# A transformer block on one core: seven instead of eight down products in the later periods of the first token half, and ScalarE accumulating part of them

## The chip, the cores and the metric

The kernel runs on one core of one Trainium2 chip. A core has five engines that run at once and each take their instructions in order: TensorE (PE, matmuls; its weight loads appear as PEld), VectorE (DVE), ScalarE (ACT), GpSimd (POOL) and SyncE (SP, which here only issues DMAs; ScalarE issues some too, shown as ACTq). The metric is the device time of one execution in microseconds (us). The profile is one more execution, recorded instruction by instruction.

## What is computed

A block of batch 1, 2048 tokens, width 576, hidden width 4608, everything in fp32: an attention part and then a gated feed-forward part, each behind a layer norm whose scale and shift come from a small conditioning vector.

```
x = A_x
h = layernorm(x) * (1 + ca) + sa
x = x + ga * attention(h)            # 32 heads, 4 segments of 512, with a memory between segments
h = layernorm(x) * (1 + cb) + sb
x = x + gb * ((silu(h @ w_gate) * (h @ w_up)) @ w_down)
```

The change lies in the feed-forward part and in the step from the attention part to it.

## The kernel before

**Numbers.** TensorE works in a reduced fp32 format. So each operand is split into a high and a low part (a ScalarE cast to the high part, then a VectorE subtraction for the low part), and a product is three matmuls: high by high, high by low, low by high.

**Order.** The feed-forward part (from line 1645) is written out by hand under a manual schedule: each engine runs its instructions in the order in which the Python code emits them. It works on two token halves, `t` = 0 and 1, of 1024 tokens, as two blocks of 512. For each half it goes through `NPR` = 18 periods, `p` = 0 to 17; a period takes 256 of the 4608 hidden columns. A period has 14 steps, `k` = 0 to 13.

**Gate and up.** Weights (two column blocks by two halves of 288 rows) times tokens (two halves of 288 by two blocks) is a 2 by 2 block product. It is done with seven block products instead of eight, for gate (`z` = 0) and up (`z` = 1): 14 products, one per step, `prod` (L1422), seven matmuls of 512 columns each. `step` (L1462) follows each by its evacuation: `copy_t` and silu on ScalarE, `fin` (L1438) mostly on VectorE. The step's weights were cast five steps before (`prep_w`, L1389: a ScalarE cast and a VectorE subtraction). In half 0, step 7 takes two `prep_w` and step 8 none: the loop of line 1756 has a bound that is one larger there.

**Down.** The four activation blocks of a period are multiplied by the down weights during the next period, `prev`. There are two forms.
- `plain` (L1545): the eight block products, as 8 chunks of 12 matmuls of 288 columns, in steps 4 to 11 of half 0. VectorE adds each chunk (128 x 576) to an accumulator in SBUF. The operands are four activation blocks (`prep_a`) and four weight blocks (`prep_d`).
- `down` (L1530): seven products as 14 chunks of 6 matmuls, spread by `CH` over steps 0 to 12 (two chunks in steps 4 and 11, none in 6 and 13). VectorE adds each chunk to one of seven accumulators `acc[1..7]`. The operands are seven activation sums (`sum_a` on VectorE in steps 2 to 5) and seven weight blocks (`sum_d`). At the end `comb` (L1574) adds the accumulators up, eight adds of 128 x 1152.

`is_plain` (L1579) decides: half 0 is plain throughout, half 1 uses the seven products in periods 0 to 15 and is plain in 16 and 17. The chunks of both use two PSUM buffers `dn` in turn. The seven weight sums of half 1 are made in half 0 by GpSimd (`mul_d` in steps 4 and 5, `sum_d` in steps 6 to 9) and stored to DRAM for half 1 (line 1821, issued by ScalarE in step 12).

**Operands of half 1.** While half 0 runs, the generator `prep2` (L1262) makes the normed, transposed and split tokens of half 1: row loads, layer norm, transposes on TensorE (into the same `dn` buffers), scale and shift, block sums on GpSimd, splits, stores to DRAM. The main loop calls it once per step in steps 1 to 13 (line 1863) of every period from 1 on; what is left is run when period 17 begins.

**Remainder rows.** 32 rows of each 288 are packed apart. For two periods at a time they are loaded (`load_rb`), summed (`sum_rb`, GpSimd), split (`split_rb`, step 4), stored to DRAM by three DMAs that ScalarE issues (`store_rb`, L1377, step 6 of odd periods) and read back as `wr` by SyncE (`prep_r`, L1357).

**From attention to feed-forward** (lines 1661 to 1715). The last quarter of the output projection (`wo_m`, L861; `wo_x`, L876, VectorE adds its result to x) runs in 32 small pieces `n`, while the first operands arrive: four operand loads `load_y` of more than 1 MB each are queued on SyncE before. GpSimd runs the weight sums, memsets and the four `sum_rb(0, ...)` (n = 7 to 10); ScalarE casts (n = 12), and the subtraction follows on VectorE; `store_rb` at n = 14, `prep_r` at n = 18 and 19. The first product needs `wr`.

Of the kernel before, what the change touches and what calls it, by code (L numbers as in the profile page):

```python
# [7 lines left out]
F32 = mybir.dt.float32  # L8
# [42 lines left out]
LM = 3  # L51
G2 = range(1, 14)
WC = 4
PRIME = (0, 1, 3, 2, 5, 4, 7, 6) + tuple(range(8, 14))
# [50 lines left out]
def block(ctx: ExitStack, tc: tile.TileContext, x, wqk, wv, wo, beta, wgu, wrm, wd, c, w_mod, wm01, out):  # L105
# [1156 lines left out]
    def prep2(x2p):  # L1262
# [17 lines left out]

        xl = ha.rearrange("p a b -> p (a b)")[:, :D]
        for sn, i in ((2, 3), (3, 0), (3, 1), (3, 2), (3, 3)):
            nc.sync.dma_start(xl, xD[sn][:, i, :])
            for _ in range(5):
                yield
# [12 lines left out]
            nc.sync.dma_start(xhD[sn][:, i, :], xl)  # L1298
            yield
        for kb in range(3):  # L1300
            n = P if kb < 2 else 96
            for hv in range(2):
                for kh in range(2):
                    c0 = 288 * kh + 128 * kb
                    for b in range(2):
                        src = xhD[2 + b][:, 2 * hv:2 * hv + 2, c0:c0 + min(P, 288 - 128 * kb)]
                        if kb < 2:
                            nc.sync.dma_start(xb[:, 2 * b:2 * b + 2, :], src)
                        else:
                            for j in range(3):  # L1310
                                nc.sync.dma_start(xb[:, 2 * b:2 * b + 2, 32 * j:32 * j + 32], src)
                    for _ in range(3 if kb < 2 else 5):
                        yield
                    pt = ps.tile([P, 2, L], F32, tag="dn", name="pt", bufs=2)[:, 0].rearrange("p (a b) -> p a b", b=P)
                    for i in range(4):
                        nc.tensor.transpose(pt[:n, i, :], xb[:, i, :n], ident)
# [3 lines left out]
                    yield  # L1320
                h00, h10, h01, h11 = [ha[:n, k, 256 * b:256 * b + 256] for k in range(2) for b in range(2)]
                nc.gpsimd.tensor_tensor(t3[:n], h11, h10, op=ALU.subtract)
# [45 lines left out]
    def sum_rb(j, i):  # L1368
        sum_w(RB[j], i, nc.gpsimd)

# [135 lines left out]

    PA, acc, x11 = {}, {}, {}
    NS = [4] + [7] * (NPR - 3) + [4] * 2
# [15 lines left out]
    def store(t, b, h, src, c=None):  # L1524
# [3 lines left out]
                          src[:, i0:i1])  # L1528

    def down(t, p, c):  # L1530
        m, c = POS[c // 2], c % 2
        ah, al = AP[p % 2, m]
        dh, dl = DP[p % 2, m]
        pd = ps.tile([P, 2, L], F32, tag="dn", name="pd", bufs=2)
        for i in range(2):
            tk = slice(128 * (2 * c + i), 128 * (2 * c + i) + 128)
            for k, (a, w) in enumerate(((ah, dh), (ah, dl), (al, dh))):
                nc.tensor.matmul(pd[:, i, :288], lhsT=a[:, tk], rhs=w, start=(k == 0), stop=(k == 2))  # L1538
        o = acc[m][:, 2 * c:2 * c + 2]
        if p == 0 and m not in (2, 3, 4):  # L1540
            nc.vector.tensor_copy(o, pd[:, :, :288])
        else:
            nc.vector.tensor_tensor(o, o, pd[:, :, :288], op=ALU.add)  # L1543
# [29 lines left out]

    def comb(j):  # L1574
        d, b = ((2, 1), (0, 5), (6, 1), (5, 6), (3, 5), (7, 6), (4, 7), (0, 7))[j]
        d = acc[d] if d else x11[1]
        nc.vector.tensor_tensor(d, d, acc[b], op=ALU.add)

    def is_plain(t, p):  # L1579
        return t == 0 or p >= NPR - 2  # L1580

# [18 lines left out]
    with tc.manual_schedule():  # L1600
# [79 lines left out]
        for i in range(4):  # L1680
            for h in range(2):
                for c in range(WC):
# [8 lines left out]
                    if n == 6:  # L1691
                        for z in range(2):
                            nc.gpsimd.memset(f32(R[z][96:128]), 0.0)
                        for o in ACT_OP.values():
                            nc.gpsimd.memset(f32(y[96:128, o, 4]), 0.0)
                    if 7 <= n < 11:
                        sum_rb(0, n - 7)
                    elif n == 12:
                        split_rb(0)
                    elif n == 14:  # L1700
                        store_rb(0)
                    elif n in (18, 19):
                        prep_r(0, 0, n - 18)
                    if n == 24:
# [18 lines left out]
        p6 = ExitStack()  # L1723
        new_acc(accp, (2, 3, 4, 5))
        load_d(0, 0)
        seq = [(p, z, m) for t in range(2) for p in range(NPR) for z in range(2) for m in MP]
# [8 lines left out]
        for t in range(2):  # L1735
            for p in range(NPR):
# [4 lines left out]
                if t == 0 and p == 1:  # L1741
                    p7.close()
                    x2p = pool(p6, "x2p")
                    g2 = prep2(x2p)
                if t == 0 and p == NPR - 1:
                    run(g2)
                    p6.close()
                    accq = pool(p4, "acq")
                    new_acc(accq, (1, 6, 7))
                if last:  # L1750
                    load_x11(1)
                chunk = 0
                for k in range(14):
# [8 lines left out]
                    while acts:  # L1762
                        acts.pop(0)()
                    if dl and k in HP:
                        y_here(6 + HP.index(k))
# [16 lines left out]
                    else:  # L1782
# [15 lines left out]
                        elif dl and k in (6, 7):  # L1798
                            mul_d(p, k - 6, nc.vector)
                        elif not dl and k in (4, 5):  # L1800
                            mul_d(p, k - 4)
                        if dl and 9 <= k < 13:
                            for j in (0, 1):
# [30 lines left out]
                    elif prev is not None:  # L1834
# [8 lines left out]
                        for _ in range(CH[k]):  # L1843
                            down(*prev, chunk)
                            chunk += 1
                    if last and 1 <= k < 9:
                        comb(k - 1)
                    if p == 0 and (t, k) in RS:
# [5 lines left out]
                    elif k >= 7:  # L1854
                        if p == 0 and k < 9:
# [78 lines left out]
```

## Time and profile before

| | |
|---|---|
| three runs | 1802.44, 1805.81, 1807.12 us (median 1805.81) |
| the profiled execution | 1806.4 us, its span 1804.5 us |
| granted TensorE clock, mean | 0.996 |
| busy share of the span | PE 98%, PEld 84%, DVE 78%, ACT 51%, POOL 26% |
| DMA | 309.84 MB, mean 172 GB/s |
| end of the attention part, first feed-forward product | the product starts at 550.87 us |
| feed-forward half 0, periods 1 to 17 | about 576 to 1176 us |
| feed-forward half 1 | about 1176 to 1804 us |

How to read it: a row of the engine table is time in which the engine had an instruction running. Matmuls overlap, so the time from one start to the next tells more than the length of one. "SPq" and "ACTq" rows are DMA issues, which are not counted as busy but hold the queue of their engine.

The second half of the page's strips (40 slices of 45 us) for the feed-forward part reads 9 throughout for PE, 7 to 8 for DVE in half 0 and 8 to 9 in half 1, 3 to 5 for ACT, and for POOL 3 to 5 in half 0 and 0 in half 1.

### The profile page before, as it was taken

What the parts mean: (1) busy time and instruction counts of PE and PEld (TensorE: products, weight loads), DVE (VectorE), ACT (ScalarE), POOL (GpSimd) and SP (SyncE); (2) the same over time, 40 slices, a digit from 0 to 9 for tenths busy, and PEclk for the clock granted to TensorE, in tenths of its full rate; (3) what the DMA queues carried; (4) which work ended last, traced back from release to release, by engine and by line L of the source; (5) the groups of instructions that cost most, each with busy time, mean ns of one, the idle gap of its engine ahead of it and who ended that gap; (6) DMA issues with size and microseconds to landing.
All of it is one profiled execution on the core that took longest, in us unless ns stands there. A gap on an engine that the chain in (4) does not pass through costs nothing.

```text
span 1804.5 us, 31293 instructions
## 1 busy us (share of the span) xinstructions
PE 1774.5 (98%) x11053; PEld 1511.6 (84%) x11053; DVE 1403.4 (78%) x3215; ACT 924.0 (51%) x2010; POOL 469.0 (26%) x752
## 2 busy tenths in 40 slices
PE   8999999999989999999999999999999999999999
PEld 5888866767767888888888888888888888888888
DVE  7567588999967776777777776568888888898886
ACT  6344577778855444444444443344544544544542
POOL 2100146555680443454353443100000000000000
PEclk9999999999998999999999999999999999999999
DMA  8678765577668555555654553594324324324331
GB/s 304 223 239 280 235 197 177 171 196 213 194 215 290 167 193 193 183 189 165 211 167 147 185 161 130 178 302 144 106 81 131 108 80 131 108 80 131 108 104 53
DMA packets 149188, 309.84 MB, mean 172 GB/s; under 512 B 28184, under 2 KB 60376, under 8 KB 147240
## 3 DMA queue, kind: packets, MB, share of 16 engines
q1 hardware_dynamic: 134824, 253.98, 46.4%
q10 hardware_dynamic: 14208, 53.86, 7.6%
q8 instruction: 88, 1.44, 0.3%
q14 instruction: 68, 0.56, 0.1%
HBM read 193.73 MB, written 113.33 MB: 170 GB/s over the span
## 4 chain that ended last, share of the span: by engine, by line
PE 79%; DMA 3%; DVE 2%; POOL 1%; issue 0%; ACT 0%; SPq 0%; ACTq 0%; DVEq 0%; POOLq 0%
PE A L1429 25%; PE pd L1557 14%; PE C L1429 13%; PE pd L1538 10%; PE B L1429 6%; PE av L766 3%; PE pw L874 2%; PE s L711 2%; PE s L740 2%; DMA y<-yD 1%; PE pn L1010 1%; DVE junk L211 1%; PE px L788 1%; PE pw L951 1%; DMA woraw<-in_wo_dram 0%
## 5 line engine op out<-in xcount | busy, mean ns | idle before, releaser
L1429 PE MATMUL A<-y,wh 128*128 128x512 f32 x1152 | 404.0, 391 | 0.7 <-DMA y<-yD 0.5
L1429 PEld LDWEIGHTS A<-y,wh 128*128 128x128 f32 x1152 | 216.7, 188 | 41.0 <-ACT sg L1445 0.7
L1567 DVE TENSOR_TENSOR acc<-acc,pd 128x576 f32<-128x576 f32 x156 | 117.5, 753 | 161.6 <-PE pd L1557 160.4
L1394 DVE TENSOR_TENSOR wl<-O,wh 128x256 fp32r<-128x256 f32 x504 | 235.3, 472 | 5.2 <-ACT wh L1393 4.7
L211 DVE CUSTOM_DVE_ANT_0 junk<-s,tri 128x384 bf16<-128x384 f32 (+3 forms) x512 | 218.5, 486 | 23.3 <-PE s L711 9.5
L1429 PE MATMUL A<-y,wl 128*128 128x512 f32 x576 | 224.7, 390 | 0.0
L1543 DVE TENSOR_TENSOR acc<-acc,pd 128x576 f32<-128x576 f32 x216 | 162.3, 752 | 54.8 <-PE pd L1538 49.7
L1429 PE MATMUL C<-y,wh 128*128 128x512 f32 x576 | 203.2, 393 | 0.0
L1393 ACT CAST wh<-O 128x256 fp32r<-128x256 f32 x504 | 197.4, 405 | 3.1 <-DVE xr L879 1.5
L1557 PE MATMUL pd<-dh,ah 128*128 128x288 f32 x640 | 189.8, 297 | 0.5 <-DVE x L1561 0.5
L1557 PE MATMUL pd<-dh,al 128*128 128x288 f32 x640 | 188.2, 294 | 0.0
L1557 PE MATMUL pd<-dl,ah 128*128 128x288 f32 x640 | 188.1, 294 | 0.0
L1498 ACT CAST ah<-sg 128x512 fp32r<-128x512 f32 x192 | 119.4, 622 | 68.6 <-DVE sg L1453 63.2
L1384 POOL TENSOR_TENSOR O<-O 128x256 f32<-128x256 f32 x132 | 108.9, 839 | 146.1 <-DMA O<-in_wgu_dram 59.2
L747 ACT ACTIVATE Pt<-s 128x512 f32<-128x512 f32 x256 | 135.5, 599 | 22.0 <-PE s L740 12.2
L1499 DVE TENSOR_TENSOR al<-sg,ah 128x512 fp32r<-128x512 f32 x192 | 136.6, 712 | 11.2 <-ACT ah L1498 10.7
L1538 PE MATMUL pd<-dh,ah 128*128 128x288 f32 x448 | 132.9, 297 | 0.0
L1538 PE MATMUL pd<-dl,ah 128*128 128x288 f32 x448 | 131.9, 294 | 0.0
L1538 PE MATMUL pd<-dh,al 128*128 128x288 f32 x448 | 131.2, 293 | 0.0
L1557 PEld LDWEIGHTS pd<-dl,ah 128*128 128x128 f32 x640 | 121.1, 189 | 6.7
L1557 PEld LDWEIGHTS pd<-dh,ah 128*128 128x128 f32 x640 | 120.2, 188 | 6.8 <-DVE x L1561 0.8
L1429 PEld LDWEIGHTS C<-y,wh 128*128 128x128 f32 x576 | 108.0, 188 | 19.4
(415 smaller groups left out, 4251.1 us busy)
## 6 DMA issues: line engine op xcount, KB each, us to landing
wr<-rD SPq DMA_DIRECT2D x213, 112.0 KB
O<-in_wgu_dram SPq DMA_DIRECT2D x36, 512.0 KB
O<-oD SPq DMA_DIRECT2D x36, 512.0 KB
oD<-O ACTq DMA_DIRECT2D x34, 512.0 KB
ks<-kD SPq DMA_DIRECT2D x64, 216.0 KB
qs<-qD SPq DMA_DIRECT2D x64, 216.0 KB
O<-in_wgu_dram SPq DMA_DIRECT2D x36, 384.0 KB
y<-yD SPq DMA_DIRECT2D x11, 1024.0 KB
```

The costliest lines, as they stand in the source:

```text
L211: nc.vector.tensor_tensor_reduce(junk[:, :n], bank[:, o:o + n], tri[:, L - n:], 1.0, -3e38, op0=ALU.add, op1=ALU.max, accum_out=mcol[u][0] ...
L747: nc.scalar.activation(pt[:, h], bank, AF.Exp, scale=SCALE)
L1384: eng.tensor_tensor(o[:, d], o[:, a], o[:, b], op=op)
L1393: nc.scalar.copy(wh, o)
L1394: later.append(lambda: nc.vector.tensor_tensor(wl, o, f32(wh), op=ALU.subtract))
L1429: nc.tensor.matmul(bank, lhsT=a, rhs=b, start=(first and n == 0), stop=(n == 6), skip_group_check=not first)
L1498: nc.scalar.copy(ah, src)
L1499: later.append(lambda: nc.vector.tensor_tensor(al, src, f32(ah), op=ALU.subtract))
L1538: nc.tensor.matmul(pd[:, i, :288], lhsT=a[:, tk], rhs=w, start=(k == 0), stop=(k == 2))
L1543: nc.vector.tensor_tensor(o, o, pd[:, :, :288], op=ALU.add)
L1557: nc.tensor.matmul(pd[:, i, :288], lhsT=a[:, tk], rhs=w, start=(k == 0), stop=(k == 5))
L1567: nc.vector.tensor_tensor(o, o, pd[:, :, :288], op=ALU.add)
```

## The change

1. In half 0 the down product uses the form with seven products from period `P7` = 7 to period 15 (nine periods); 0 to 6 and 16, 17 stay plain. Accumulators 1, 6 and 7 are allocated at period 7 instead of 17, half 0 gets an accumulator of its own for product 5 (`acc5[0]`), and `comb` now also runs in period 17 of half 0.
2. In half 0, five of the 14 chunks (`PA7` = 1, 3, 7, 9, 13) are accumulated without VectorE: at the start of the chunk's step ScalarE copies the accumulator into the PSUM buffer (`down_new`), the matmuls add to it, and ScalarE copies the result back. In the first use of a new accumulator there is nothing to copy in.
3. In those periods `mul_d` moves from steps 4 and 5 to step 2, `sum_d` from steps 6 to 9 to steps 3 and 4.
4. `prep2` must be done before period 7: it is called twice per step in periods 1 to 6, its loads use two buffers in turn and are issued further ahead, and the waiting steps between are fewer.
5. Before the feed-forward part, `sum_rb(0, ...)` runs on VectorE at n = 9, the cast at n = 10, the store at n = 12, `prep_r` at n = 17 and 18.

The diff, without the body of `prep2` (whose numbers of steps are told in the prediction where they are used):

```diff
+P7 = 7
+PA7 = (1, 3, 7, 9, 13)
...
     def sum_rb(j, i):
-        sum_w(RB[j], i, nc.gpsimd)
+        sum_w(RB[j], i, nc.gpsimd if j else nc.vector)
...
+    def down_acc(t, c):
+        m, c = POS[c // 2], c % 2
+        return (acc5[t] if m == 5 else acc[m])[:, 2 * c:2 * c + 2]
+
+    def down_new(t, p, c):
+        pd = PD[c] = ps.tile([P, 2, L], F32, tag="dn", name="pd", bufs=2)
+        if t == 0 and c in PA7 and (p > P7 or POS[c // 2] in (2, 3, 4)):
+            nc.scalar.copy(pd[:, :, :288], down_acc(t, c))
+
     def down(t, p, c):
-        m, c = POS[c // 2], c % 2
+        m, q = POS[c // 2], c % 2
         ah, al = AP[p % 2, m]
         dh, dl = DP[p % 2, m]
-        pd = ps.tile([P, 2, L], F32, tag="dn", name="pd", bufs=2)
+        pd = PD.pop(c)
+        new = p == (0 if t else P7) and m not in (2, 3, 4)
+        on_act = t == 0 and c in PA7
+        first = new or not on_act
...
-                nc.tensor.matmul(pd[:, i, :288], lhsT=a[:, tk], rhs=w, start=(k == 0), stop=(k == 2))
-        o = acc[m][:, 2 * c:2 * c + 2]
-        if p == 0 and m not in (2, 3, 4):
+                nc.tensor.matmul(pd[:, i, :288], lhsT=a[:, tk], rhs=w, start=(first and k == 0), stop=(k == 2),
+                                 skip_group_check=not first)
+        o = down_acc(t, c)
+        if on_act:
+            nc.scalar.copy(o, pd[:, :, :288])
+        elif new:
             nc.vector.tensor_copy(o, pd[:, :, :288])
...
     def is_plain(t, p):
-        return t == 0 or p >= NPR - 2
+        return p >= NPR - 2 or t == 0 and p < P7
...
-                    if 7 <= n < 11:
-                        sum_rb(0, n - 7)
+                    if n == 9:
+                        for j in range(4):
+                            sum_rb(0, j)
+                    elif n == 10:
+                        split_rb(0)
                     elif n == 12:
-                        split_rb(0)
-                    elif n == 14:
                         store_rb(0)
-                    elif n in (18, 19):
-                        prep_r(0, 0, n - 18)
+                    elif n in (17, 18):
+                        prep_r(0, 0, n - 17)
...
-                if t == 0 and p == NPR - 1:
+                if t == 0 and p == P7:
                     run(g2)
                     p6.close()
                     accq = pool(p4, "acq")
                     new_acc(accq, (1, 6, 7))
+                    acc5[0] = xp.tile([P, 4, 288], F32, tag="xs", name="acc50")
...
                     while acts:
                         acts.pop(0)()
+                    if prev is not None and not is_plain(*prev):
+                        for j in range(CH[k]):
+                            down_new(*prev, chunk + j)
...
-                        elif not dl and k in (4, 5):
+                        elif not dl and is_plain(t, p) and k in (4, 5):
                             mul_d(p, k - 4)
+                        elif not is_plain(t, p) and k in (2, 3, 4):
+                            for j in (0, 1):
+                                if k == 2:
+                                    mul_d(p, j)
+                                else:
+                                    sum_d(p, 2 * k - 6 + j)
...
-                        if not dl and k in (6, 7, 8, 9) and p < NPR - 2:
+                        if not dl and k in (6, 7, 8, 9) and p < P7:
                             sum_d(p, k - 6)
...
-                    if last and 1 <= k < 9:
-                        comb(k - 1)
+                    if p == NPR - 1 and 1 <= k < 9:
+                        comb(t, k - 1)
...
-                    if t == 0 and k in G2 and p > 0:
+                    if t == 0 and k in G2 and 0 < p < P7:
+                        next(g2, None)
                         next(g2, None)
```

More of the change, by code (lines that the diff above doesn't have):

```diff
@@ L1279, in opr, with load_row @@
             yield
[L1281 to L1285, printed above, removed]
+        xl2 = x2p.tile([P, D], F32, tag="xl2", name="xl2")
+        xls = (ha.rearrange("p a b -> p (a b)")[:, :D], xl2)
+        rows = ((2, 3), (3, 0), (3, 1), (3, 2), (3, 3))
+        def load_row(j):
+            sn, i = rows[j]
+            nc.sync.dma_start(xls[j % 2], xD[sn][:, i, :])
+        load_row(0)
+        load_row(1)
+        for _ in range(5):
+            yield
+        for j, (sn, i) in enumerate(rows):
+            xl = xls[j % 2]
             st = x2p.tile([P, 2, 6], F32, tag="st3", name="st3")
@@ L1299, in prep2, with load @@
             yield
+            if j < 3:
+                load_row(j + 2)
+            for _ in range(3):
+                yield
+        xbs = (xb, xl2[:, :L].rearrange("p (a b) -> p a b", b=P))
+        def load(j):
+            kb, hv, kh = j // 4, j // 2 % 2, j % 2
+            c0 = 288 * kh + 128 * kb
+            for b in range(2):
+                src = xhD[2 + b][:, 2 * hv:2 * hv + 2, c0:c0 + min(P, 288 - 128 * kb)]
+                if kb < 2:
+                    nc.sync.dma_start(xbs[kh][:, 2 * b:2 * b + 2, :], src)
+                else:
+                    for r in range(3):
+                        nc.sync.dma_start(xbs[kh][:, 2 * b:2 * b + 2, 32 * r:32 * r + 32], src)
+        load(0)
+        yield
+        load(1)
+        for _ in range(5):
+            yield
         for kb in range(3):
@@ L1303, in prep2 @@
                 for kh in range(2):
[L1304 to L1313, printed above, removed]
                     pt = ps.tile([P, 2, L], F32, tag="dn", name="pt", bufs=2)[:, 0].rearrange("p (a b) -> p a b", b=P)
                     for i in range(4):
-                        nc.tensor.transpose(pt[:n, i, :], xb[:, i, :n], ident)
+                        nc.tensor.transpose(pt[:n, i, :], xbs[kh][:, i, :n], ident)
                     c = 3 * kh + kb
@@ L1320, in prep2 @@
                     yield
+                    j = 4 * kb + 2 * hv + kh + 2
+                    if j < 12:
+                        load(j)
                 h00, h10, h01, h11 = [ha[:n, k, 256 * b:256 * b + 256] for k in range(2) for b in range(2)]
@@ L1505, in sum_a @@
         nc.vector.tensor_tensor(PA[d], PA[a], PA[b], op=op)
-    PA, acc, x11 = {}, {}, {}
+    PA, acc, x11, acc5 = {}, {}, {}, {}
     NS = [4] + [7] * (NPR - 3) + [4] * 2
@@ L1572, in plain, with comb @@
                 return lambda: store(t, b, h, d)
[L1574 to L1577, printed above, removed]
+    def comb(t, j):
+        d, b = [x11[1] if t and n == 0 else acc[5] if n == 0 else acc5[t] if n == 5 else acc[n]
+                for n in ((2, 1), (0, 5), (6, 1), (5, 6), (3, 5), (7, 6), (4, 7), (0, 7))[j]]
+        nc.vector.tensor_tensor(d, d, b, op=ALU.add)
     def is_plain(t, p):
-        return t == 0 or p >= NPR - 2
+        return p >= NPR - 2 or t == 0 and p < P7
     flows = {}
@@ L1724, in block @@
         new_acc(accp, (2, 3, 4, 5))
+        acc5[1] = acc[5]
         load_d(0, 0)
@@ L1854, in block @@
                     elif k >= 7:
-                        if p == 0 and k < 9:
+                        if t and p == 0 and k < 9:
                             for j in ((0, 1, 2) if k == 7 else (3,)):
```

4 lines of the change are left out of this document (3 added, 1 removed).

## The prediction

> **What bounds the kernel now.** I read the page's first table, then who waited for whom on TensorE, then the engines by stretch.
>
> ```profile
> span 1804.5 us, 31293 instructions
> PE 1774.5 (98%) x11053; PEld 1511.6 (84%) x11053; DVE 1403.4 (78%) x3215; ACT 924.0 (51%) x2010; POOL 469.0 (26%) x752
> ```
> ```profile
> PE A L1429 <- DMA y<-yD: 0.5, 1, 0.5
> PE A L1429 <- ACT tb L1458: 0.2, 1, 0.2
> ```
> ```profile
> core 0: us, PE busy (x) PEld busy (x) DVE busy (x) ACT busy (x) POOL busy (x), PEclk, DMA share, GB/s
> 857.70:893.70 36.00, 36.00 (x204) 32.06 (x203) 25.39 (x42) 16.85 (x37) 15.12 (x16) 1.00 0.60 191
> 893.70:928.60 34.90, 34.90 (x195) 31.04 (x195) 26.69 (x45) 15.37 (x37) 16.34 (x20) 1.00 0.55 172
> 1463.60:1497.20 33.60, 33.60 (x183) 29.54 (x183) 29.18 (x56) 16.41 (x38) 0.00 (x0) 1.00 0.35 105
> ```
>
> The middle fence is everything that TensorE waited for between 556 and 1750 us: 0.7 us. The third has two periods of half 0 and one of half 1: TensorE is busy all the time, at full clock. So the feed-forward part is bound by TensorE, and fewer matmuls shorten it as long as the others keep up. A period's length is read best from the chain that ended last, where its pairs of products without a chunk between (x14) come once per period:
>
> ```profile
> 1070.86 3.17 PE A L1429 x14
> 1105.82 3.17 PE A L1429 x14
> 1140.86 3.17 PE A L1429 x14
> ...
> 1463.59 3.23 PE A L1429 x14
> 1497.18 3.23 PE A L1429 x14
> ```
>
> Plain: 70.00 / 2 = 35.00 us. Seven products: 33.59 us.
>
> **The change part by part.** *Down products.* Nine periods (7 to 15) lose 12 of 96 down matmuls: 35.00 - 33.59 = 1.41 us each, **-12.7 us**, if nothing else is late.
>
> *VectorE* in such a period does what it does in half 1, 29.18 us, less five evictions, plus the remainder rows' subtraction every second period, plus its slower running beside GpSimd. That stays near 29 of 33.6 us: hidden.
>
> *ScalarE* gets ten copies of 128 x 576. The trace has none; the nearest rows:
>
> ```profile
> L1543 DVE TENSOR_TENSOR acc<-acc,pd 128x576 f32<-128x576 f32 x216 | 162.3, 752 | 54.8 <-PE pd L1538 49.7
> L1475 ACT COPY B<-A 128x512 f32<-128x512 f32 x51 | 29.1, 571 | 49.5 <-PE A L1429 49.5
> L1374 ACT CAST RH<-RB 128x896 fp32r<-128x896 f32 x3 | 2.8, 945 | 0.0
> L1577 DVE TENSOR_TENSOR acc<-acc,acc 128x1152 f32<-128x1152 f32 x6 | 8.1, 1354 | 0.1
> ```
>
> A copy costs between 0.57 us (512 columns) and 0.945 us (896); I take 0.65, near the first. Ten are 6.5 us on top of 16.41: on average ScalarE is not full. But the copy into PSUM is a new wait: TensorE stands in front of its chunk until ScalarE, in order, has come to it, and behind that chunk stand all later products. ScalarE has the time of the step's own product, 1.6 us, less what is queued ahead. So I went through the five steps; step 7 is the bad one. Half 1 shows its timing (start and length, TensorE first):
>
> ```profile
> 1463.43 0.40 PE L1429 MATMUL A<-y,wh 128*128 128x512 f32 x1
> 1465.06 0.39 PE L1429 MATMUL A<-y,wh 128*128 128x512 f32 x1
> 1466.66 0.30 PE L1538 MATMUL pd<-dh,ah 128*128 128x288 f32 x1
> ```
> ```profile
> 1465.25 0.60 ACT L1442 ACTIVATE sg<-A 128x512 f32<-128x512 f32 x1 [0.99 <-PE A L1429]
> 1465.75 0.40 ACT L1393 CAST wh<-O 128x256 fp32r<-128x256 f32 x1
> 1466.91 0.57 ACT L1475 COPY B<-A 128x512 f32<-128x512 f32 x1 [0.77 <-PE A L1429]
> ```
>
> Step 6 (from 1463.43) has no chunk, so step 7's product follows at 1465.06 and chunk 7 at 1466.66. ScalarE must first do the silu of step 6's product, which can't start before 1465.25; then the weight casts; only then comes the copy. In half 0 step 7 has two casts, and in odd periods the three DMA issues of `store_rb` stand behind that silu:
>
> ```profile
> 1016.17 0.60 ACT L1442 ACTIVATE sg<-A 128x512 f32<-128x512 f32 x1 [1.36 <-PE A L1429]
> 1016.23 0.81 ACTq L1380 DMA_DIRECT2D rD<-RH  x2
> 1017.09 0.63 ACTq L1380 DMA_DIRECT2D rD<-RB  x1
> 1017.75 0.43 ACT L1418 CAST dh<-dr__13735 128x288 fp32r<-128x288 f32 x1 [0.99 <-issue]
> 1018.10 0.71 ACT L1393 CAST wh<-O 128x256 fp32r<-128x256 f32 x2
> ```
>
> Even period: silu 1465.25, casts from 1465.75 for 0.71 (the next starts 0.1 before their end), copy from 1466.37 to 1467.02, and an estimated 0.06 for the signal: chunk 7 starts at 1467.08, **0.4 us** late. Odd period: ScalarE is free 1017.75 - 1016.17 = 1.58 us after the silu's start instead of 0.50: **1.5 us** late. In period 7's own products chunk 7 starts a new accumulator and needs no copy, so eight of the nine periods pay: 4 x 0.4 + 4 x 1.5 = **+7.6 us** (7.0 with copies of 0.57; 10 with 0.945). The delay is not made good, because the silu of the next period again hangs on TensorE. The other four steps have room. The tightest is step 1:
>
> ```profile
> 1484.66 0.71 ACT L1393 CAST wh<-O 128x256 fp32r<-128x256 f32 x2
> ```
> ```profile
> 1485.86 0.29 PE L1538 MATMUL pd<-dh,ah 128*128 128x288 f32 x1
> ```
>
> One of these casts belongs to step 1, so the copy runs from 1484.98 to 1485.63, 0.2 us ahead of chunk 1.
>
> *`mul_d`, `sum_d` earlier.* Issue and use of the weights now:
>
> ```profile
> 896.11 1.38 SPq L1401 DMA_DIRECT2D dr__12551<-in_wd_dram  x2
> ```
> ```profile
> 900.81 1.54 POOL L1407 TENSOR_TENSOR dr__12551<-dr__12551,gbB 128x576 f32<-128x576 f32 x1 [11.60 <-DVE wl L1394]
> ```
>
> At step 2 GpSimd will wait for the load, at most 4.7 us after its issue in step 1; behind it stand `sum_d` and the gate/up sums. Two `mul_d` (3.1 us) and four `sum_d` (half the columns, so about as much in all) end some 11 us after the issue, in step 5; first use is step 7. Cost nothing.
>
> *`comb` in period 17*: 8 x 1.35 = 10.8 us more on VectorE. Half 1's last period does the same between plain chunks, and TensorE's waits above name none. Cost nothing; if it came through, a few us.
>
> *`prep2`*: 5 + 5 x 5 + 6 + 6 x 17 = 138 calls are needed and 6 x 13 x 2 = 156 are there: it ends in period 6 and nothing is left to run at once. The transposes themselves only move (36.00 against 34.90 us above: 1.1 us for eight of them). New is that a pair can fall into one step (calls 37 and 71, steps 6 and 10): its second transpose needs the buffer of the chunk just done, whose eviction takes 0.75 us and its signals an estimated 0.25 (0.19 from TensorE's 1465.06 to ScalarE's 1465.25), less 0.5 for the first four transposes. Twice 0.5: **+1.0 us** (0 to 3).
>
> *The start.* Here the trace has its one big stall:
>
> ```profile
> 531.00:535.00 4.00, 4.00 (x32) 3.81 (x30) 1.53 (x3) 0.00 (x0) 3.94 (x6) 1.00 1.03 329
> 535.00:542.50 7.50, 0.04 (x1) 0.00 (x0) 1.46 (x2) 0.96 (x2) 4.83 (x11) 0.72 1.03 317
> 542.50:548.50 6.00, 6.00 (x25) 6.00 (x26) 3.65 (x8) 4.01 (x8) 0.00 (x0) 0.50 1.01 357
> 548.50:552.30 3.80, 3.80 (x25) 3.31 (x24) 2.89 (x8) 1.76 (x4) 0.00 (x0) 1.00 0.94 352
> 552.30:554.50 2.20, 0.12 (x1) 0.00 (x0) 1.23 (x3) 0.00 (x0) 0.00 (x0) 1.00 0.90 279
> 555.40:558.80 3.40, 3.40 (x10) 2.63 (x9) 2.23 (x5) 2.61 (x7) 0.00 (x0) 0.51 1.00 273
> ```
> ```profile
> DVE RB L1375 <- ACT RH L1374: 8.4, 1, 8.4
> PEld pw L874 <- DVE xr L879: 7.7, 1, 7.7
> ```
>
> VectorE waits 8.4 us in front of the remainder rows' subtraction, because GpSimd comes to `sum_rb` late; the output projection's add stands behind it, and TensorE behind that (7.5 us). With `sum_rb` on VectorE this chain goes. What is late next: the first product still needs `wr`, which is stored and reloaded, and TensorE would only come to that wait sooner. The DMA share is 0.90 to 1.03 from 531 to 554.5: the engines are full, and the operand loads queued ahead of `wr` and the store move the same bytes in either order. So `wr` lands where it did, within 1 or 2 us: **0**, bounds -7 (the store 7 us earlier, all passed on) and +2. The clock stands at 0.50 and 0.51 after the two waits. The Trainium skill (TensorE: Matmul & The Clock Gate, "What's actually happening") says that an idle window of about 3.4 us halves the clock and a busy one restores it; the rows agree, and by it one long wait of some 12 us would cost 1.7 to 3.4 us of slow matmuls behind it instead of 1.7: the sum would be about 1 us higher.
>
> *Sum* against the profiled execution: 1806.4 - 12.7 + 7.6 + 1.0 + 0 = 1802.3. That execution is 0.6 above the median of the three runs (1805.81), so 1801.7: **1802 us**, own range 1798 to 1806.
>
> **The rivals.** *The copies are in time.* If ScalarE comes to step 7's copy 1.5 us earlier than I read it, all 12.7 us remain: 1805.8 - 12.7 + 1.0 = 1794. For it: with the copies ScalarE is busy 22.9 of 33.6 us, so there is idle time to shift into. Against it: the order of the rows above.
>
> *The start gains.* If the store's earlier issue lets `wr` land up to 7 us sooner: 1802 - 7 = 1795. For it: on the chain the stall is real. Against it: the DMA share.
>
> *Slower: ScalarE is late at three more copies.* The room in steps 1, 9 and 12 is 0.2 to 0.4 us, ending with ScalarE one cast (0.4 us) later than in half 1, as half 0's DMA issues in steps 11 to 13 could make it. Then TensorE waits a copy there each time: 3 x 8 x 0.65 = 15.6 us, 1818. Against it: ScalarE's idle times of 0.77 and 0.99 us in the rows.
>
> *Slower: VectorE and GpSimd.* `mul_d` and `sum_d` now run beside `sum_a`. If 1 us of that reaches TensorE per period, 9 us: 1811. Against it: VectorE has lost five evictions just there. The Trainium skill (SBUF — State Buffer, "Who interferes with whom") says that a VectorE operation with two SBUF inputs and a GpSimd one that reads SBUF exclude each other for the whole instruction.
>
> *It does not do what it says*: leftover `prep2` at period 7 with TensorE waiting; the count of calls excludes it.
>
> **How the numbers follow.** Forecast 0.47, copies in time 0.20, start 0.14, late copies 0.10, VectorE 0.05, rest 0.04. 0.3% is 5.4 us, about what a measurement of this kernel can tell from no change: faster means under 1800.4. Faster: 0.20 + 0.13 + a quarter of the forecast (0.11) = 0.44; slower 0.10 + 0.05 + 0.01 = 0.16; same 0.40. The range 1793 to 1809 leaves out the two slower rivals and a sum of both gains.
>
> **What would show it.** Right: periods 9 to 16 of half 0 alternate near 34.0 and 35.1 us, TensorE's waits name the new copy line with about 0.4 and 1.5 us; no wait for the projection's add at 535, and one of about 12 us for `wr`, with the first product still ending near 554.5. Wrong: periods of 33.6 throughout, waits at other steps, or the first product done before 551.

## The result and the profile after

The changed kernel takes 1814.76 us (median of six runs, 1810.24 to 1818.77); the kernel before, beside it, 1806.46 us. The ratio is 1.0053, with a 95% interval of 1.0039 to 1.0067: slower by 0.5%, where the prediction had 1802 us and a range of 1793 to 1809. The page of the profiled execution begins:

```profile
span 1813.1 us, 31431 instructions
PE 1765.0 (97%) x10945; PEld 1494.4 (82%) x10945; DVE 1495.2 (82%) x3326; ACT 994.7 (55%) x2151; POOL 485.3 (27%) x748
```

TensorE did what the change promised: 108 matmuls fewer and 9.5 us less work. But its share fell, and the span grew by 8.6 us. So TensorE waits now. Before, all its waits between 556 and 1750 us came to 0.7 us. The same list for the changed kernel, from 520 us on (engine, tile and line, whom it waited for: us in total, times, the longest; two waits of the attention part left out, marked by dots):

```profile
PE A L1453 <- DMA wr<-rD: 10.4, 1, 10.4
PE pd L1576 <- ACT pd L1563: 8.6, 8, 1.8
PE pd L1576 <- DVE acc L1584: 4.9, 7, 1.1
PE pw L876 <- DVE xr L881: 1.9, 3, 1.0
PE A L1453 <- ACT B L1499: 1.5, 1, 1.5
...
PE pt L1337 <- DVE acc L1608: 0.8, 2, 0.4
PE A L1453 <- ACT tb L1482: 0.7, 1, 0.7
...
```

The first row is the wait for `wr` that the prediction expected. The second is the copy into PSUM of step 7, expected too, eight times. The third was in no term of the forecast, only among its rivals: chunk 6 (step 5) waits for VectorE, seven times. The fourth is the projection's add, down from 7.5 us. The last three belong to `prep2` in periods 1 to 3; of these only `pt`, the transposes, was costed.

These waits are somewhat smaller than what they cost, because the next matmul also starts slowly. Below, a cost is what two starts of TensorE lie apart beyond the usual 0.23 us of a product's matmuls. The first wait at step 5 shows it (start, length):

```profile
846.50 0.39 PE L1453 MATMUL C<-y,wr 128*128 128x512 f32 x1
847.96 0.40 PE L1576 MATMUL pd<-dh,ah 128*128 128x288 f32 x1 [1.07 <-DVE acc L1584]
```

The page would count 1.07 us; the starts are 1.46 us apart, so the cost is 1.23. Added up in this way, step 5 costs 6.0 us, step 7 9.9 us, two waits for ScalarE in periods 1 and 2 2.6 us and the two transposes 1.1 us: 19.6 us. Two waits of the kernel before that are gone cost it 1.0 us. Against 12.7 us of removed matmuls, with the first product ending 1.1 us later, this makes 19.6 - 1.0 - 12.7 + 1.1 = +7.0 us of the 8.6; the other 1.6 us stay unexplained.

The lengths of the periods, from the pairs of products without a chunk in the chain that ended last:

```profile
902.60 3.18 PE A L1453 x14
...
937.38 3.18 PE A L1453 x14
...
974.07 3.18 PE A L1453 x14
...
1009.17 3.18 PE A L1453 x14
```

A period takes 34.78, then 36.69, then 35.10 us. The prediction had 34.0 and 35.1 in turn: the alternation is there, and each is 0.8 to 1.6 us longer than that.

Why is VectorE late at step 5? Here are VectorE and, behind it, GpSimd from step 2 to step 4 of one period:

```profile
871.48 0.69 DVE L1476 TENSOR_TENSOR cu<-C,tb 128x512 f32<-128x512 f32 x1
872.21 1.73 DVE L1477 TENSOR_TENSOR sg<-cu,sg 128x512 f32<-128x512 f32 x1
873.87 1.67 DVE L1418 TENSOR_TENSOR wl<-O,wh 128x256 fp32r<-128x256 f32 x1
...
876.33 0.74 DVE L1584 TENSOR_TENSOR acc<-acc,pd 128x576 f32<-128x576 f32 x1
```
```profile
871.96 3.29 POOL L1431 TENSOR_TENSOR dr__12374<-dr__12374,gbB 128x576 f32<-128x576 f32 x2 [8.31 <-DMA dr__12374<-in_wd_dram]
...
875.82 4.43 POOL L1436 TENSOR_TENSOR dr__12374<-dr__12374 128x288 f32<-128x288 f32 x4
```

While GpSimd runs the two `mul_d` (871.96 to 875.25), one VectorE instruction takes 1.73 us and the next 1.67, which ends at 875.54, just behind the second `mul_d`; the same line took 0.69 us at 866.17, and the same subtraction 0.42 at 870.53. Yet the eviction at 876.33 takes its usual 0.74 us, although GpSimd's `sum_d` runs beside it: one of its inputs, `pd`, lies in PSUM. VectorE's groups over eight periods show the same (columns: busy us, mean ns); ahead of them the same groups in half 1 of the kernel before, where GpSimd does nothing:

```profile
L1394 DVE TENSOR_TENSOR wl<-O,wh 128x256 fp32r<-128x256 f32 x209 | 87.4, 418 | 0.0
...
L1505 DVE TENSOR_TENSOR sg<-sg 128x512 f32<-128x512 f32 x60 | 41.0, 684 | 0.0
L1453 DVE TENSOR_TENSOR sg<-cu,sg 128x512 f32<-128x512 f32 x30 | 20.8, 693 | 1.0
```
```profile
L1418 DVE TENSOR_TENSOR wl<-O,wh 128x256 fp32r<-128x256 f32 x110 | 64.8, 600 | 0.0
...
L1529 DVE TENSOR_TENSOR sg<-sg 128x512 f32<-128x512 f32 x32 | 32.5, 1015 | 0.0
L1477 DVE TENSOR_TENSOR sg<-cu,sg 128x512 f32<-128x512 f32 x16 | 18.1, 1129 | 0.5
...
L1473 DVE TENSOR_TENSOR sg<-A,sg 128x512 f32<-128x512 f32 x8 | 5.5, 683 | 0.0
```

With both inputs in SBUF the means grow from 418 to 600, 684 to 1015 and 693 to 1129 ns; with one in PSUM (`sg<-A,sg`) it stays 683. Multiplied by the counts: 110 x 0.18 + 32 x 0.33 + 16 x 0.44 = 38 us, nearly 5 us of VectorE in each of eight periods, from all of GpSimd's work there (the gate and up sums too). The Trainium skill (SBUF — State Buffer, "Who interferes with whom") says that a VectorE instruction with two SBUF inputs contends with a GpSimd instruction that reads SBUF, and that one with at most one, outside its two-port modes, does not. The rows agree on both.

### The profile page after: what moved, and what is told of

Same layout as the page of the kernel before. It is cut to its first block, busy times and chain, and to the rows that moved or that the text cites. A ratio compares the mean times of both kernels' runs of the same rounds, so it can differ in the third digit from the quotient of the medians.

```text
span 1813.1 us, 31431 instructions
## 1 busy us (share of the span) xinstructions
PE 1765.0 (97%) x10945; PEld 1494.4 (82%) x10945; DVE 1495.2 (82%) x3326; ACT 994.7 (55%) x2151; POOL 485.3 (27%) x748
## 4 chain that ended last, share of the span: by engine, by line
PE 73%; DVE 6%; DMA 3%; ACT 2%; issue 1%; POOL 1%; ACTq 0%; SPq 0%; DVEq 0%; POOLq 0%
PE A L1453 22%; PE pd L1576 14%; PE C L1453 11%; PE pd L1598 7%; PE B L1453 6%; PE av L768 3%; PE pw L876 2%; PE s L713 2%; PE s L742 2%; DVE wl L1418 1%; DVE sg L1529 1%; PE pn L1012 1%; DMA rD<-RB 1%; DVE acc L1584 1%; DMA wr<-rD 1%
## 5 line engine op out<-in xcount | busy, mean ns | idle before, releaser
L1584 DVE TENSOR_TENSOR acc<-acc,pd 128x576 f32<-128x576 f32 x292 | 218.3, 750 | 66.2 <-PE pd L1576 59.6
L1576 PE MATMUL pd<-dh,ah 128*128 128x288 f32 x700 | 209.4, 299 | 13.5 <-ACT pd L1563 8.6
L1576 PE MATMUL pd<-dl,ah 128*128 128x288 f32 x700 | 206.1, 294 | 0.0
L1576 PE MATMUL pd<-dh,al 128*128 128x288 f32 x700 | 205.1, 293 | 0.0
L1523 DVE TENSOR_TENSOR al<-sg,ah 128x512 fp32r<-128x512 f32 x219 | 160.7, 734 | 10.9 <-ACT ah L1522 10.7
L1522 ACT CAST ah<-sg 128x512 fp32r<-128x512 f32 x219 | 136.0, 621 | 54.0 <-DVE sg L1477 38.9
L1576 PEld LDWEIGHTS pd<-dh,al 128*128 128x128 f32 x700 | 132.1, 189 | 0.0
L1453 PE MATMUL A<-y,wr 128*128 128x512 f32 x288 | 113.9, 395 | 10.4 <-DMA wr<-rD 10.4
L1453 PEld LDWEIGHTS A<-y,wl 128*128 128x128 f32 x576 | 108.3, 188 | 15.4
L1469 ACT ACTIVATE sg<-sg 128x512 f32<-128x512 f32 x73 | 46.2, 633 | 124.5 <-DVE sg L1468 124.5
```

What stands on the lines that cost most here:

```text
L1453: nc.tensor.matmul(bank, lhsT=a, rhs=b, start=(first and n == 0), stop=(n == 6), skip_group_check=not first)
L1522: nc.scalar.copy(ah, src)
L1523: later.append(lambda: nc.vector.tensor_tensor(al, src, f32(ah), op=ALU.subtract))
```

## The experiments

Theory 1: ScalarE comes late to the copy of step 7. Theory 2: GpSimd beside VectorE makes VectorE late at step 5. Theory 3: the normalisation of `prep2` blocks ScalarE in period 1. Theory 4: the start is worth nothing. The rivals stand in the expectations. Each ratio is against the kernel before, run on the same chip; the last three columns are what TensorE's waits at these steps cost, in us between its starts, summed over the nine periods.

| run | median us | ratio, 95% interval | step 4/5 | step 7 | step 9 |
|---|---|---|---|---|---|
| changed kernel | 1814.8 | 1.0053 (1.0039 to 1.0067) | 6.0 | 9.9 | 0 |
| e1_chunk7_vectore | 1808.2 | 1.0029 (1.0018 to 1.0040) | 6.0 | 0 | 6.0 |
| e2_store_on_sync | 1811.6 | 1.0042 (1.0028 to 1.0055) | 5.1 | 7.5 | 0 |
| e3_no_gpsimd_prep | 1805.1 | 1.0002 (0.9990 to 1.0013) | 0 | 7.9 | 0 |
| e4_prep_on_vectore | 1807.5 | 1.0016 (1.0007 to 1.0025) | 0 | 7.9 | 0 |
| f1_copy_one_step_early | 1801.5 | 0.9968 (0.9956 to 0.9980) | 0 | 0 | 3.5 |
| f2_norm_later | 1799.4 | 0.9956 (0.9941 to 0.9971) | 0 | 0 | 3.5 |
| f3_start_undone | 1800.1 | 0.9960 (0.9945 to 0.9975) | 0 | 0 | 3.5 |
| f4_all_on_vectore | 1797.3 | 0.9945 (0.9930 to 0.9960) | 0.3 | 0 | 0 |
| g1_vectore_with_gpsimd | 1807.6 | 1.0007 (0.9997 to 1.0017) | 10.3 | 0 | 0 |
| g2_f4_norm_later | 1792.9 | 0.9925 (0.9912 to 0.9938) | 0 | 0 | 0 |
| g3_g2_start_undone | 1795.2 | 0.9940 (0.9925 to 0.9956) | 0 | 0 | 0 |
| g4_e4_store_on_sync | 1803.7 | 0.9985 (0.9975 to 0.9996) | 0 | 3.5 | 1.6 |

The waits don't account for every ratio. For f4, all its waits and the removed matmuls together give 9.5 us under the kernel before, and the ratio 9.9; for e4 they give 1.4 us under it, and the ratio 2.9 us over it. So what two ratios from different chips lie apart is read here as good to some 4 us.

### e1: chunk 7 back on VectorE

```diff
-PA7 = (1, 3, 7, 9, 13)
+PA7 = (1, 3, 9, 13)
```

> Edit: the accumulation of chunk 7 (step 7) goes back from ScalarE to VectorE; the four others stay with ScalarE. Theory 1 (the copy into PSUM at step 7 is late): the changed kernel's TensorE waits 8.6 us for that copy, eight times, so these waits go and the time falls by 8 to 10 us against the changed kernel, from 1814.8 to about 1806, while the waits for VectorE in front of chunk 6 (4.9 us) stay. Rival (VectorE has no room for a fifth more eviction of 0.75 us, and the order behind step 7 then slips): the waits for VectorE grow by what the others fall, and the time stays within 3 us of 1814.8.

Faster by 0.24% than the changed kernel, some 4 us, not 8 to 10. TensorE's waits:

```profile
PE pd L1576 <- DVE acc L1584: 4.9, 7, 1.1
PE pd L1576 <- ACT pd L1563: 4.7, 8, 0.8
```

Step 5 is untouched, as theory 1 said, and step 7's wait is gone. But eight new waits for the same copy line appear: now it is chunk 9's, at step 9. ScalarE's rows of one period show why:

```profile
886.62 0.63 ACT L1469 ACTIVATE sg<-sg 128x512 f32<-128x512 f32 x1 [0.60 <-DVE sg L1468]
887.16 0.63 ACT L1563 COPY pd<-acc 128x576 f32<-128x576 f32 x1
```

The copy stands behind the silu of step 8's sum, and that silu waits for VectorE. While step 7 held TensorE up, this second copy had the time. Neither theory had this: the delay taken away at one copy came back in part at the next one.

### e2: the store issued by SyncE

```diff
-            nc.scalar.dma_start(rD[j][c], v)
+            (nc.sync if j else nc.scalar).dma_start(rD[j][c], v)
```

> Edit: the three DMA issues that store the split remainder rows go from ScalarE's queue to SyncE's; nothing else. Theory 1a (in odd periods these issues, 1.6 us, stand ahead of step 7's copy): the four waits of 1.8 to 2.0 us at step 7 fall to those of the even periods, 0.4 us, that is -6.3 us, to about 1808.5. Rival (the silu of step 6, and not the issues, sets when the copy starts): the odd periods keep more than 1.2 us, and the time moves by less than 3 us. If SyncE, waiting in front of the store, holds back the loads of weights behind it, new waits for wh or wr appear on TensorE, which neither has.

The odd waits fall from 1.98 to 1.40 us, not to 0.4, and the time by 0.11%, 2 us, not 6.3; no wait for weights appears. The rival was nearer: ScalarE (first row) and VectorE (the others) in the odd period show what holds the copy now:

```profile
884.31 0.63 ACT L1469 ACTIVATE sg<-sg 128x512 f32<-128x512 f32 x1 [2.94 <-DVE sg L1468]
```
```profile
882.59 1.08 DVE L1399 TENSOR_TENSOR RB<-RB,RH 128x896 fp32r<-128x896 f32 x1
883.59 0.68 DVE L1468 TENSOR_TENSOR sg<-C,tc 128x512 f32<-128x512 f32 x1
```

ScalarE stood idle for 2.94 us in front of the silu of step 5's sum, because VectorE, behind by the stretched instructions, made that sum only after the remainder rows' subtraction. With this delay in place, the DMA issues are only a third of the odd wait. Theory 1a fails for the changed kernel; g4 tests it without that delay.

### e3 and e4: GpSimd freed in steps 2 to 5

e3 leaves `mul_d` and `sum_d` out in periods 7 to 15 and fills the summed slots by loads, so its values differ; e4 gives the work to VectorE, in steps 3 to 6:

```diff
-                        elif not is_plain(t, p) and k in (2, 3, 4):
-                            for j in (0, 1):
-                                if k == 2:
-                                    mul_d(p, j)
-                                else:
-                                    sum_d(p, 2 * k - 6 + j)
+                        elif not is_plain(t, p) and k in (3, 4, 5, 6):
+                            if k < 5:
+                                mul_d(p, k - 3, nc.vector)
+                            else:
+                                for j in (0, 1):
+                                    sum_d(p, 2 * k - 10 + j, nc.vector)
```

> Left out: from period 7 to 15 of half 0 the down weights are neither scaled nor summed (mul_d and sum_d); the three summed slots are filled by a load of weights instead, so the values differ and the number of matmuls, casts and evictions does not. Theory 2 (VectorE is late with the eviction of chunk 4 because GpSimd's mul_d and sum_d in steps 2 to 5 stretch its instructions beside them, 0.69 to 1.73 us and 0.42 to 1.67 us in one period): the waits in front of chunk 6 go, -5 to -6 us, to about 1809, and the instructions have their usual length there. Rival (VectorE has too much work of its own in steps 2 to 5: four sum_a, four evictions, the casts' second halves and the remainder rows' subtraction): the waits in front of chunk 6 stay above 4 us in all.

> Edit: mul_d and sum_d of the down weights from period 7 on are done by VectorE itself (mul_d at steps 3 and 4, sum_d at 5 and 6) instead of by GpSimd: about 2 x 0.75 + 4 x 0.43 = 3.2 us more of VectorE's own work in each of nine periods. Theory 2 (what hurts is GpSimd beside VectorE, about 4 to 5 us of stretching a period): VectorE's busy time in such a period falls or stays, and the waits in front of chunk 6 shrink, 1809 to 1813. Rival (VectorE's own work is what is too much): the waits grow, above 1818.

Between 840 and 1150 us TensorE waits for one thing only, the same in both; this is e4's answer:

```profile
PE pd L1576 <- ACT pd L1563: 6.6, 8, 1.3
```

The waits at step 5 are gone, and step 7's odd ones fall from 1.98 to 1.49 us, so more than expected comes back. e3 is 9 us faster than the changed kernel by the ratios, e4 6.7. In e4, VectorE does some 3.3 us more work of its own per period, and its groups are short again:

```profile
L1418 DVE TENSOR_TENSOR wl<-O,wh 128x256 fp32r<-128x256 f32 x113 | 47.7, 433 | 0.0
...
L1529 DVE TENSOR_TENSOR sg<-sg 128x512 f32<-128x512 f32 x32 | 25.7, 803 | 0.0
L1477 DVE TENSOR_TENSOR sg<-cu,sg 128x512 f32<-128x512 f32 x16 | 12.0, 749 | 0.6
```

VectorE's busy time in the whole page falls from 1495.2 to 1480.9 us although it took over work: without the moved work on GpSimd, VectorE's other work takes (1495.2 - 1480.9 + 9 x 3.3) / 9 = 4.9 us less per period. Theory 2 holds, against its rival (too much work of VectorE's own), and in e3 with one and a half times its expected size: VectorE's lateness also lengthened step 7. Not tested is the same work on GpSimd at other steps.

### f1: the copy one step earlier

The edit is on top of e4's.

```diff
+                        early = prev[0] == 0 and k in (6, 7)
-                        for j in range(CH[k]):
+                        for j in range((k == 6) if early else CH[k]):
                             down_new(*prev, chunk + j)
```

> Edit: as e4_prep_on_vectore, and the copy of chunk 7's accumulator into PSUM is issued one step earlier, at step 6 (which has no chunk), ahead of the silu of step 6's product, the two casts and the store's issues. Theory 1 (step 7's wait is the queue ahead of the copy, nothing else): the eight waits there (1.49 and 0.39 us, 7.8 us in all in that kernel) are gone, and the time falls from its 1807.5 to about 1800. Rival (ScalarE's queue is simply full, and what comes behind the copy slips instead: the copy of A into B at step 7, or the copy at step 9, as when chunk 7 went to VectorE): new waits for ScalarE of 0.4 to 1 us appear at steps 8 to 10, and the time stays above 1804.

Step 7's waits are gone, so what caused them is the queue ahead of the copy. The rival is right about what follows: in the four odd periods the copy of chunk 9 is late by 0.88 us.

```profile
PE pd L1576 <- ACT pd L1563: 2.9, 4, 0.7
```

The time is between the two expectations, 8.7 us below e4 by the ratios; the waits in the table give 4.4 of it.

### f2: the normalisation later

The edit is on top of f1's.

```diff
-            yield
+            for _ in range(3):
+                yield
             nc.scalar.activation(xl, xl, AF.Identity, scale=rs[:, 0:1], bias=nb[:, 0:1])
...
-            for _ in range(3):
-                yield
+            yield
```

> Edit: as f1_copy_one_step_early, and in the row part of the operand preparation two of the five pauses of a row are moved ahead of ScalarE's normalisation. Theory 3 (at double pace the normalisation stands in ScalarE's queue before GpSimd has its scale ready, and TensorE loses 2.0 and 0.9 us behind it in period 1): both waits go, -2.5 to -2.9 us against f1. Rival (GpSimd is as late two calls on): the waits stay, or move to another copy.

Here is ScalarE in period 1 of the changed kernel, and GpSimd beside it:

```profile
599.06 0.87 ACT L1307 ACTIVATE xl<-xl,nb,rs 128x576 f32<-128x576 f32 x1 [3.86 <-POOL nb L1305]
...
600.43 0.57 ACT L1499 COPY B<-A 128x512 f32<-128x512 f32 x1
```
```profile
597.12 1.02 POOL L1436 TENSOR_TENSOR dr__8997<-dr__8997 128x288 f32<-128x288 f32 x1
...
598.76 0.26 POOL L1305 TENSOR_SCALAR nb<-mv,rs 128x1 f32<-128x1 f32 x1
```

ScalarE waits 3.86 us for a shift that GpSimd makes only after weight sums; behind it stand the casts and the copy of A into B, and TensorE behind that copy. In f2 the long wait is gone and the other, in period 2, is down from 0.84 to 0.43 us, nearly as theory 3 said. The time falls by 0.12%, about 2 us, which the intervals of f1 and f2 don't separate; the trace decides.

### f3 and g3: the start undone

f3 is f2 and g3 is g2 (below), each with

```diff
-        sum_w(RB[j], i, nc.gpsimd if j else nc.vector)
+        sum_w(RB[j], i, nc.gpsimd)
...
-                    if n == 9:
-                        for j in range(4):
-                            sum_rb(0, j)
-                    elif n == 10:
+                    if 7 <= n < 11:
+                        sum_rb(0, n - 7)
+                    elif n == 12:
                         split_rb(0)
-                    elif n == 12:
+                    elif n == 14:
                         store_rb(0)
-                    elif n in (17, 18):
-                        prep_r(0, 0, n - 17)
+                    elif n in (18, 19):
+                        prep_r(0, 0, n - 18)
```

> Edit: as f2_norm_later, with the start put back to that of the kernel before: the first remainder rows are summed by GpSimd at products 7 to 10, split at 12, stored at 14 and reloaded at 18 and 19. Theory 4 (the transfers set when the first product ends, so the start neither gained nor lost): within 1.5 us of f2, and the first product ends between 551 and 556 us in both. Rival (the long wait with the half clock behind it costs more than the two short ones, as the trace of the changed kernel suggests with 555.9 against 554.5): f3 is 1 to 3 us faster than f2.

> Edit: as g2_f4_norm_later with the start of the kernel before. Theory 4 (the start is worth nothing either way): within 1.5 us of g2. Rival (f3's span, 4 us shorter than f2's, is the start's cost): 2 to 4 us faster than g2.

With the old start TensorE waits for the projection's add again (7.6 us) and less for `wr`; this is g3:

```profile
PE pw L876 <- DVE xr L881: 7.6, 1, 7.6
PE A L1453 <- DMA wr<-rD: 4.0, 1, 4.0
```

The first product ends (the next one starts) at 555.4 and 554.4 us in these two and at 554.9 in the kernel before; with the new start it ends, over eleven traces, between 551.0 and 557.5, at 554.5 in the mean (f2's, at 556.2, lies just outside what was expected). By the times f3 is 0.04% slower than f2 and g3 0.15% slower than g2, both within the intervals. So the start neither loses nor gains anything that these runs can tell, as theory 4 said; the expectation of 1.5 us was exceeded once, by g3's 2.3 us.

### f4 and g1: no accumulation on ScalarE

f4 is e4, g1 the changed kernel, each with

```diff
-PA7 = (1, 3, 7, 9, 13)
+PA7 = ()
```

> Edit: as e4_prep_on_vectore, and none of the fourteen accumulations is done by ScalarE: VectorE gets five evictions of 0.75 us more in each of nine periods. Theory (VectorE, freed of GpSimd beside it, is near full with its own work: 1480.9 us busy in all): the waits for ScalarE at step 7 go (-7.8), but VectorE gets 3.8 us more per period and TensorE waits for it in front of several chunks, 1 to 3 us per period: 1809 to 1825. Rival (VectorE has the room): no such waits, about 1800.

> Edit: the changed kernel with all fourteen accumulations on VectorE, and nothing else: GpSimd still does mul_d and sum_d in steps 2 to 5. Theory 2 (GpSimd beside VectorE is what makes VectorE late): step 7's waits for ScalarE go (-9.9), but VectorE, 3.8 us fuller and still stretched, is later in front of chunk 6 and perhaps other chunks: waits for it of 9 to 20 us in all where the changed kernel has 4.9 to 6, and about 1808 to 1820, some 10 to 20 us above f4_all_on_vectore, which differs by GpSimd's work alone. Rival (the five copies on ScalarE were the only fault): waits for VectorE stay near 5 us and the time comes near 1804.

f4 went against the expectation and with its rival: no wait of TensorE in these periods but one of 0.3 us, and the fastest of its four. VectorE is full, and still TensorE doesn't wait for it (ScalarE does, and has the time):

```profile
881.10:915.00 33.90, 33.77 (x184) 29.38 (x183) 33.53 (x62) 16.34 (x38) 8.54 (x9) 1.00 0.53 172
915.00:948.70 33.70, 33.70 (x184) 29.64 (x183) 33.45 (x61) 17.24 (x39) 8.99 (x12) 1.00 0.44 140
```

After the window and its length come PE, PEld and VectorE: 33.53 of 33.90 us. g1 has the same accumulations with GpSimd at work beside them, and other waits:

```profile
PE pd L1576 <- ACT ah L1522: 6.0, 8, 0.8
...
PE pd L1576 <- DVE acc L1584: 1.8, 4, 0.6
```

The first is an activation operand whose sum VectorE made late, the third the eviction in front of a chunk of step 4: 10.3 us between TensorE's starts, at the lower end of what theory 2 expected, and the time just under it. g1 to f4 is who does `mul_d` and `sum_d`, and at which steps, alone: 0.62%, 11 us. And g1 is 0.46% (8 us) faster than the changed kernel: even with GpSimd in the way the five accumulations on ScalarE lose time.

### g4: the store on SyncE, VectorE in time

The edit is e2's on top of e4.

> Edit: as e4_prep_on_vectore, and the store of the remainder rows issued by SyncE as in e2_store_on_sync. With VectorE in time, what is left of step 7's odd-period wait (1.49 us) is the prediction's sum: about 1.1 us for the three DMA issues and 0.4 us for silu and casts. Theory 1a: the odd waits fall to 0.4 to 0.5 us, -4 us in all, to 1803.5. Rival (the remainder rows' subtraction on VectorE, 1.1 to 1.6 us ahead of the sum whose silu stands before the copy, holds ScalarE as long as the issues do): they stay above 1 us.

The odd waits at step 7 fall from 1.49 to 0.39 us: 1.1 us for the three issues, 0.4 for silu and casts, as theory 1a said. A part returns at step 9, four times 0.40 us.

### g2: the faster kernel

g2 is f4 with f2's edit.

> Edit: as f4_all_on_vectore, and the normalisation two pauses later as in f2_norm_later. The trace of f4 has 2.5 us of waits for ScalarE's copies in period 1, of which f2's edit took all but 0.4 us: 1795.2. If period 1's waits don't set the time, 1797.

It takes 1792.9 us, against 1795.2 expected, ratio 0.9925 (0.9912 to 0.9938): 13.5 us under the kernel before, and by the ratios 23 under the changed one. All its waits from 556 to 1760 us:

```profile
PE pt L1337 <- DVE acc L1608: 1.1, 3, 0.4
PE A L1453 <- ACT tb L1482: 0.3, 1, 0.3
```

So within the interval the nine periods bring the 12.7 us that were computed for them, and of the change's other costs only these small waits are left.

## Why the prediction was wrong

The step that failed is *VectorE* together with *`mul_d`, `sum_d` earlier*: "That stays near 29 of 33.6 us: hidden" and "Cost nothing".

- **Removed matmuls, -12.7 us**: right. Without waits (f4, g2) the periods take the 33.6 us that half 1 showed, and g2 gains 13.5 us (11 to 16 by the interval).
- **VectorE, costed at nothing**: wrong, and the largest miss. Its load was taken from half 1, where GpSimd does nothing, and the slower running beside GpSimd got words and no number. In the changed kernel VectorE is busy for 33.37 us of a period of 36.60:

```profile
866.00:902.60 36.60, 33.95 (x183) 29.27 (x182) 33.37 (x51) 22.82 (x49) 15.53 (x15) 1.00 0.45 153
```

  And a load averaged over a period says little about step 5: the `sum_a` of the seven products, four evictions and GpSimd's moved work all fall into steps 2 to 5. It cost 6.0 us at step 5 and, because a silu in ScalarE's queue waits for VectorE's sum, another 2 us at step 7. e3 and e4 took both away. The prediction had this mechanism as a rival with 1811 us and a chance of 0.05. The argument against it, five evictions fewer "just there", counted 3.8 us of relief against nearly 5 us of stretching that was never priced; and of the five chunks only chunk 3 lies in steps 2 to 5, the others in steps 1, 7, 9 and 12. The prices could have been had: the trace of the kernel before has line 1453 (`sg<-cu,sg`) at 693 ns in half 1 and at 967 ns between 1000 and 1210 us, in half 0 with GpSimd at work.
- **Step 7's copy, +7.6 us**: right in mechanism and, taken alone, in size: with VectorE in time (e4) it costs 1.49 and 0.39 us (the last of the even ones 0.72) where 1.5 and 0.4 were predicted, 7.9 us in all. g4 confirms its parts. In the changed kernel it was 9.9 because of VectorE. The room that the prediction gave step 9 was there only while step 7 held TensorE up (e1, f1).
- **`prep2`, +1.0 us**: the transposes cost 1.1 us, as computed. That the rest of the double pace costs nothing was wrong: two waits cost 2.6 us, and f2 takes 2.1 of them away. The normalisation is handed to ScalarE one call after GpSimd gets its work, which is now half a step instead of a whole one.
- **The start, 0**: right within what the runs tell. The wait for `wr` was 10.4 us instead of 12, and the half clock behind it lasted 3.7 us:

```profile
555.30:559.00 3.70, 3.64 (x9) 2.91 (x10) 1.12 (x2) 2.54 (x6) 0.00 (x0) 0.50 1.00 261
```

  In the kernel before, matmuls ran slowly for 3.4 us behind a wait of 2.2 us (0.51 from 555.40 to 558.80) and for 6.0 us behind one of 7.5 us (0.50 from 542.50 to 548.50). So the slow stretch doesn't follow the length of the wait in these traces, and they bear out the idle window of the prediction's rule less plainly than its "the rows agree" says: the second wait was of 2.2 us only.

Put together: 1802.3 + 6.0 + 2.3 + 2.6 + 0.1 + 1.1 (this trace's start) - 1.0 (the waits of the kernel before that are gone) = 1813.4, against 1814.8 measured in the profiled execution; 1.4 us stay open. The unknown that was priced at nothing, without bounds, is the one that decided; the rival that did bound it (1 us per period, 1811 us) lay outside the range.

## What to carry to other kernels

When work is moved to GpSimd's free time, look at which VectorE instructions run beside it: those with two SBUF inputs were stretched here, so that 7.7 us of moved work cost VectorE 4.9 us per period, and doing it on VectorE itself (3.3 us) was the cheaper way. A hand-off to an idle engine in the middle of a tight loop is judged by its place in that engine's queue, not by its busy share: ScalarE at 55% was late at step 7, then at step 9, while VectorE at 99% held TensorE up by 0.3 us in all, since what TensorE needs from it was due later. Load a stage by the step where its work piles up, not by the mean of a period.

## What the runs showed that was not expected

VectorE can be busy for 33.5 of 33.7 us of a period without a single TensorE wait (f4): with two `dn` buffers in turn, an eviction only has to end before the second chunk after it. An instruction of VectorE that meets GpSimd can take four times as long (0.42 to 1.67 us for 128 x 256), and one with an input in PSUM, beside GpSimd too, takes none longer (0.74 us). ScalarE's copies of 128 x 576 between SBUF and PSUM, for which the prediction took 0.65 us, took 0.63 to 0.65 us in both directions.
